# One load of 128 rows for each late half tile's queries, and a new table of issue times with a new order

## The chip, the cores and the metric

The kernel runs on one core of a Trainium2 chip. The core has a matrix engine (TensorE, PE in the profile), a vector engine (VectorE, DVE), an engine for activations (ScalarE, ACT), GpSimd (POOL), and a sync engine (SyncE, SP) whose queue issues all transfers of this kernel. Sixteen DMA engines move the data between memory and the core. The metric is the device time of one execution in microseconds, the median of several runs.

## What is computed

Local attention with block summaries, followed by a layer norm and a two-layer network with a residual:

```python
# q, k, v: (4, 8, 768, 64) float32
k_sum = k.reshape(B, H, nb, block, D).max(axis=3)     # block = 32
v_sum = v.reshape(B, H, nb, block, D).mean(axis=3)
scores_l = scale * np.matmul(q, k.transpose(0, 1, 3, 2))
mask_l = np.abs(pos[:, None] - pos[None, :]) < window  # window = 16
scores_s = scale * einsum('bhsd,bhnd->bhsn', q, k_sum) + np.log(block)
a = softmax over [where(mask_l, scores_l, -1e9), scores_s]
attn = np.matmul(a, concat([v, v_sum]))
x = attn.transpose(0, 2, 1, 3).reshape(B, S, 512)
xn = (x - mean) / sqrt(var + 1e-06) * g_ln
out = x + np.maximum(xn @ w_ch1, 0.0) @ w_ch2          # 512 -> 2048 -> 512
```

## The kernel before

**Tiles.** The 4 x 768 rows are 24 tiles T of 128 rows. A half tile t = 2T + hh holds four of the eight heads. The first batch (T = 0 to 5) takes an early path with float32 matmuls. The other three batches (T = 6 to 23, so 36 half tiles) take the late path, in which queries, keys, values and probabilities are split into a high and a low float16 part.

**Queries on the late path.** `load_q` (L602) loads the queries of one half tile. In memory they are 64 rows (the head dimension) of 512 float32 values (four heads by 128 positions), 2 KB a row. The tile `qs` has 128 rows, and its two halves hold the same 64 rows: `qhl` needs in its rows 0 to 63 the high part and in its rows 64 to 127 the low part. Two transfers of 64 rows, 128 KB each, fill `qs` from one source. Then ScalarE writes `qhl` as float16 of the scaled queries (128 x 512), and VectorE replaces rows 64 to 127 with the rest (64 x 512). `qs` has one buffer, so the next half tile's load waits until VectorE has read it. While batch 1's statistics are taken, that buffer also holds some of their loads (`stg`, L457). `qhl` has one buffer for each of two half tiles in turn.

**The rest of a half tile.** `load_k` (L615) loads keys (tile `ksg`) and splits them; `load_v` loads values (tile `vst`, three transfers) and splits them. `heads` (L640) makes the scores of both half tiles of T and the products with the values of tile T - 2, in one unbroken run of TensorE. `late_softmax` (L687) takes the maximum, the exponentials and their split, and transposes the probabilities with a DMA (tile `pt`). `batch_k`, `batch_q` and `batch_v` (L467 to L538) take the statistics of the next batch from loads into the one buffer `bst`. Layer norm transposes its result with a DMA too (tile `xt`), and `g1` and `g2` do the two layers (groups `h` and `a` in the profile) in groups of two tiles.

**Who sets the order.** Nothing is issued as the code is run through. A class `Plan` records every instruction with its dependences; `schedule` places them on five engines with a model of their times, and `issue` (L336) then emits them in order of the modelled start. The emitted order is fixed for each engine, SP's queue among them. Two inputs of the model matter here:

- `ISSUE`, `TURN` and `MOVE` (L114 on): the time that SP takes to issue a transfer (470 ns for every plain one, 1250 ns for a transpose) and, by the rows and bytes per row of its tile on the core, the time that it holds the DMA engines and the time from there to landing.
- `ORDER` (L54): 781 numbers, one for each step of the kernel (`load_q(12)`, `heads(6)` and so on), found by annealing, and added to the ranks by which `schedule` picks the next instruction (L346).

Every recorded instruction has line L356 in the profile, since it is emitted there. Groups are told apart by tile names.

Of the kernel before, what the change touches and what calls it, by code (L numbers as in the profile page):

```python
# [51 lines left out]
LAG = 2  # L52

ORDER = (  # L54
    "K>7dwc;Wy5hVTFXRmuPVjGF)d5XJxhoVEY|^{W5>ezgDpK(hb;yA%KbFy8<F(xw0ZzRCapFy8<FG_3#s!JGg8y)pm*AngDD=llQvM7sa~pVR;U"
    "qVNCzYC!-1Ug!V+)jR+Iwxs|6><0h<3oQTugvI~=zOeuQPX_=155fQcTZjMuji~?sfC>NrwI~1pvF-"
    "o=xWxbeDWw1Zhavy~c)kDs0ZIS>!ZrW^1p5E~n704_?~nig^$h?30zUu%OWyzgR?YwaOs)U_^RWN_eWw5az@z{FZ@mBi?uGyVUZem2ai#zNg{c"
    "4k^_Tzus-ge?T$lg<OsxO^%dP+aoRa_lkoW)pC!zoU>Z1Su42J*zf3pAol!yQS*tP%v8Ib?~CzSvHptt}3q2d4kHt+xc`@R4F7R~?vz0LpsH{A"
    "dKnyCN(dC&j<MEC#yq5J>;Hs}BULDm2NV9Edg@6rGNz8L@j-Sq$ev#J08LJR-^*i!%iIUWE2-o5|-"
    "nCAcgSgHU2Q#t?uV$A>l)BXSdK@<Q0=`;WU>qh_p4_E*I+0+03N8JDa9k>7g#GwEGn+X5_f13aQ$;to!&{O~bqq+b8UhV(?0doKVZ`l9;lm7qz"  # L60
    "Sk(Xj56S=k?JfWSl1cyowH5#X1^oa2e>wmF=EVR1?-"
    "u|7#@+w_(~<xG8w~&e1|t9fLr?$!W=jA7jcfn_5P1Lq5uE@3nLq#l=UM;&+}{8H9R&aYvj6}8v2p+azx@CIp#}f|WVrwTcA5YG=N|w7r=|b@Nk"
    "0Gp1ik<NJCy(bap3>|TCo5BUC#giIr;zpC6539A;JIusmTBTO%wnCpUwaO1q%QGS?T}(UI_pI!}kCGKh^*Ln;rlFxVHcQ>l6S0%@hCt)bIcQ5e"
    "EPOSqlIF`&s}1>0kf=1^EB}E4csvfS~{X+3ElPstN!A&C37(cjy2Ay^H_<$IAczzn%a8PMrV$Dq#Qs54`{XfY<;3?YsZ~jQ0Qkrv?B3IpF{QjO"
    "PFU$F2YW!T<mN;Kl#{xTydC6XpN^CK~_%!t?+CW8VM&m?QuIdKUlyG`;`-"
    "TgU(ZJ0t)ARZjo_R^k8u7^MII$F~3f>H`1(wkH4pD_j5ooCN>?CJq1q*NOlCI{E+q(!&4$JKF#MS<3(asmuTWix&U@^4S0XI<x=(c%=XTq80!E"
    "1dRXx_x1n(6<PoQ!1(|FlZ*fVR@(pnU>pDdArt@rJvsmY15^M2S3m#&(JBA{YbyW%3v2)YrYZmcWdZ;I1aJTVNiF~YKX?EDNBjT(2<`v>L|Xs="
    "Tp<7eHaP$QnX&)>;4c6G-a7yQX(a#v82|tOinIU!ZV><gB+dW-+@1gb9q<4Dz1{!+_DBE#EhPW|txNy_sLKEUKm-"
    "5)%&GtXdBp$!4!r;W8Uz3UBgFszR{#J1&gTFB@7(|YU=08OMz#O{PwM~w3L^jjyD<O&QWyXLEFJ&=&o2M~GHL(-#>oHw>|p=^B-"
    "a1`LgxSf=S2Vj1qlEEUjYCBAx;1Qdp-aFS{ncWU?%_o{0{&Cwm1L)2>t*6*2n+<#sB~REc*Zdvj6}9vp@g<Nk{+yjvD{~c-"  # L70
    "a5{Wf1@Xwr2nUur>eya!UXJUPk}`zHI;i>uvx50(t-djvD{~{!0J=Jsto6BtifH2U-9Cv`_#5w?+T}H6{Q6F+>0W7w-"
    "T6RyqIxI~o80flvSd&L02($}j)`e?0&I)c^nh3NHWvuo(aV+T{QL)baoSF24W&?=}DcIqm=d!twwA6S)8XGBp4I<6i&(vGM=^{^I}tQ1Ac$kk$"
    "YH1vmfzvcdoVRrde?$pQcX??C_naV!7;03QGV7100xg;M|k-"
    "v<By?JWQR1vCHvoX`LNnNI)!Qwab7c%T3OUG4w>L<Rr=(<%S}n9%?K3NruzoGbtUx=8>4U)=xyFaQ7mAHe_r*9-"
    "svyVw8!GNS+gDiZ(zDy{$j_ZI*FHv<3wzzP5Ww($S|T<ib;=)V8|BryO0OWXhdJ{SN1qVE6yMf?B%&msT-CqV!J2T1?`^-"
    "=%;ok0Kqd{F=ZT~7c2>^uMf$|C>(@W226$`Swobcp}|^z;A!_v`=v%O3y$yx;%--"
    "D&^;F)RQ87)1a8f6xE_@<;#x8?pcYVI%+mpV|Na3Z?)5OS}L7l)?Z1HRAvODMbJPn%)2ZWaR(<7cKw*69oVOtn~l?tP=nLysZEK650R%f(-"
    "xwozVaPLQDVvP-XxC$Lat7=(_*^E5`r-OY8stdf@;6(%Jw2vdRDdm!|*!B-"
    "a1`cL)FgXTSgd`1b$*trP$N^~(SMJ^%m!c+>y?3g!R*P^|y|2h9Kf6W0I#zUBY_=cfPv#FPL31eO2)`HTPm$UOi6m&O18%)tNuzU2S^1<wEfQq"
    "2GVUH||8(vScD1kL~doyq_Is0{!B<)Q!oR+az%(5?Uf*O~wS#i0NHHL?Hyu9g4)B&+}b@^=6L^G^T(*S-"  # L80
    "J$NWcI8@aq5nVVM8_R44!dp~?UM3IPBB_s9SLz`+0i?D_xy8m<5TD4_rU^{W5>xUv8L{3!qc6`TM6N3#F_0FM9vkc$8Rb^`zaT%rH}vc~`a?XC"
    "a+SG)iJ{@nlnn=t?YUabHBRk8p7!;%0073u%~0=obIA*28QI=lb>cAWqJ9nAm#HMal%#u@+sYt{e%&(Qz>D;xj-"
    "mX81bsm=fYLdyUDtf&9~BgX&#H^u+|+m`?TpA!H8Wc>gCTsQy#k#PV31110fN7n!UY^wkN7q0*RA-eznfh7O{VzdAMx6%LqOOF5l;U541m+Ali"
    "QcwT@lD7Z<{^|e!<r4q^@c94#NbLXr>KXt5F7^NazKZ|<sP6y&?2G^ZfDixxHH`oNye<F$8rA>*!<zs9GRgn{8sz`~P^ka^)W!e*8S4N4m!kjw"
    "^T7ZA86W@vM7aO|12+HwNHPEbjA#G=i?09wy7K@3`zinc)@%R(E<FGM`EmdNBQXE~@8JLcuP^`r&H?}cPALEY$j<-"
    "&=%D}qji~?sytV)TZVmtdNm2j+=Dq*_4JZHr@9h8oE7AY|(1`#4rJeu(^z8rtgX#bOcbNbGZ4UqdeboQ|3C{ojaGC%A{SN>DXXXF@TN?lX4GRD"
    "Oed+)I*uww+q4xj(CawSf8tDK3+Y<l)KVJX<Zn*#dzheLZT^axY!V~}i?p6Q*lurNvIxPSIYcl`<Z_)q%sG<M=VXOcD{3QSY6`BA4rM&<Dg{uG"
    "mw6p*J^rQd(Cno>^&`tmVQE&hNcSisKHbDRYk{18~iHraLgbx4!i;VyO=LrA+ftCONf29Ba;HCfn(YpWt?%V(W4p{&ITeScGL(2dEs*(Ty+r0n"
    "(RUH5T&d~q=(UJfEaE<@}FjxQp3aS79sqFv%u-O0qDwzNO^RNH^PqP325lR36h>`#Qsy6@tybS;VN4fw1v8Mn3It%~+Jf{Eup$-"
    "55{a^q9g8Kjen<fAN?$iJOpVa^VMDhRs&AR{pF5>_H%hdn>1)=}{d+7iFe=Pt2mgoQfIBNg^DUkpFk}d!MJ=OpJ;pYGU_=*4j;I;q%>c;>7@>u"  # L90
    "`?Ubg@L@T~v;9VGw&*;oJoyp#X`h>QRKi2MKlR+0bzv84b1kdFWVqvikqPOSg`F6saO^wj_Vk30YXGq(T#xeWjSQM3R5B=i6O8{_}~tiS*NW7_"
    "}!Kr;XUxhDVs-tYhak}d!M!@mFj3zPr<#JvCip&I}I16%+ADB1u29<u-cVUGX*6qEn|$5j9T!_@!(T)+SSVJiRttg8S2`1k++fx-"
    "X(Ru}*PCv^Y-L0<p>mMs7Ppwj>U94!C<A;SOvMyvn-Bs~BC88ZL?!NLFkyIcSO2Q&Zxeq8_ndKUlyD`)@!;#>d#K{5aU4jljhY#aapHB<lqv2g"
    "$Z=?nk>p+W!v$2b50HEsX^!%YAHekA|^rV;=EMF;=@<01e6Yb5{xo6i6LZ43YahB5#EpHct-"
    "4*387f<gcQaHaqM3&#Kdui^jyL0<p>dm{h<(7XTt73}~2AkqK-O1%I7RsjG2tS<lnAVvTHwe$b~eeD1Lk{<v7mZ|^$"
# [11 lines left out]
class Plan:  # L107
# [8 lines left out]
    MOVE = {
        "T": (1520.0, 550.0),
        (1, 2048): (170.0, 880.0),
        (128, 1024): (610.0, 490.0),
        (128, 1536): (680.0, 790.0),  # L120
        (128, 2048): (750.0, 880.0),
        (128, 2944): (1530.0, 960.0),
        (128, 3072): (1360.0, 1010.0),
        (128, 4096): (1770.0, 1290.0),
        (128, 576): (40.0, 2010.0),
        (24, 512): (110.0, 730.0),
        (32, 1024): (40.0, 820.0),
        (32, 2048): (40.0, 2000.0),
        (64, 1024): (220.0, 830.0),
        (64, 2048): (750.0, 770.0),  # L130
        (96, 1024): (490.0, 590.0),
        (96, 2048): (800.0, 700.0),
    }

    def __init__(self):
# [89 lines left out]
    def cost(self, engine, op, a, k, ins, outs):  # L225

        free = lambda x: math.prod(n for _, n in x.ap[1:])
        n = max(free(x) for x in ins + outs) if engine != "tensor" else free(a[0])
        if engine == "sync":
            x = (outs + ins)[0]  # L230
            size = mybir.dt.size(x.dtype)
            if "transpose" in op:
                return self.TURN, *self.MOVE["T"]
            return self.ISSUE, *self.MOVE[x.ap[0][1], free(x) * size]
        if engine == "tensor":
            dt = ins[-1].dtype
            if dt == F32R:
# [123 lines left out]
def body(ctx: ExitStack, tc, qt, qa, qe, kt, ks, va, vb, vs, g_ln, w1, w2, blocks, out):  # L361
# [5 lines left out]
    def work(tag, name, shape, dt=F32, bufs=1):  # L367
        return pl.tile(wp, shape, dt, tag, name, bufs)
# [21 lines left out]
    nc = pl  # L390
# [10 lines left out]
    sp = {}  # L401
# [199 lines left out]
    @pl.step  # L601
    def load_q(t):  # L602

        T, hh = divmod(t, 2)
        qs = stg('qs', [P, 4, P])
        for half in range(2):
            nc.sync.dma_start(qs[D * half : D * half + D], qt[T, hh])
        qhl = work(f"qhl{t % 2}", f"qhl{t}", [P, 4, P], F16)
        sc = bt["s", T // NT][:, 1:2]
        nc.scalar.activation(qhl[:], qs[:], AF.Copy, scale=sc)  # L610
        nc.vector.scalar_tensor_tensor(qhl[D:], qs[D:], sc[D:], qhl[D:], ALU.mult, ALU.subtract)
        st[t, "q"] = qhl
# [483 lines left out]
    for T in range(4, TT + LAG + 1):  # L1096
# [5 lines left out]
        b, i = divmod(T, NT)  # L1102
# [66 lines left out]
```

## Time and profile before

| | us |
|---|---|
| median of 3 runs | 632.35 |
| fastest and slowest of them | 631.36, 634.27 |
| the profiled execution | 631.18 |
| its span, first to last instruction | 629.4 |
| busy: TensorE, VectorE, ScalarE, GpSimd | 616.1, 401.6, 351.1, 147.0 |

The profile is of one execution. A group is named by its engine, its operation and the tiles that it writes and reads (`qhl<-qs`). "Busy" counts an engine's own instructions; SP's rows (SPq) are the times that its queue took to issue transfers. The chain of work is followed back from the last instruction, at each step to whatever released it. The table of stretches gives for each stretch the busy time of the engines, the granted TensorE clock, the mean busy share of the 16 DMA engines and what they moved in GB/s.

### The profile page before, as it was taken

What the parts mean: (1) busy time and instruction counts of PE and PEld (TensorE: products, weight loads), DVE (VectorE), ACT (ScalarE), POOL (GpSimd) and SP (SyncE); (2) the same over time, 40 slices, a digit from 0 to 9 for tenths busy, and PEclk for the clock granted to TensorE, in tenths of its full rate; (3) what the DMA queues carried; (4) which work ended last, traced back from release to release, by engine and by line L of the source; (5) the groups of instructions that cost most, each with busy time, mean ns of one, the idle gap of its engine ahead of it and who ended that gap; (6) DMA issues with size and microseconds to landing.
All of it is one profiled execution on the core that took longest, in us unless ns stands there. A gap on an engine that the chain in (4) does not pass through costs nothing.

```text
span 629.4 us, 14009 instructions
## 1 busy us (share of the span) xinstructions
PE 616.1 (98%) x5227; PEld 427.5 (68%) x5227; DVE 401.6 (64%) x1098; ACT 351.1 (56%) x926; POOL 147.0 (23%) x271
## 2 busy tenths in 40 slices
PE   8999999999999999999799999999999999999997
PEld 6777779885544676667377884577766756677754
DVE  4899999879668268846687465676877821171211
ACT  4898985459977257746677364565767711121100
POOL 4110302201333005403343022441433410030000
PEclk9999999999999999999799999999999999999999
DMA  9968798454797627555976426835776350011001
GB/s 285 308 175 259 237 302 231 99 159 120 192 226 166 151 73 191 155 159 134 199 209 139 95 70 125 188 83 146 176 152 151 74 120 0 1 48 23 1 25 43
DMA packets 115831, 89.52 MB, mean 142 GB/s; under 512 B 69553, under 2 KB 100273, under 8 KB 115762
## 3 DMA queue, kind: packets, MB, share of 16 engines
q1 hardware_dynamic: 115762, 88.61, 54.9%
q8 instruction: 41, 0.67, 0.4%
q14 instruction: 28, 0.23, 0.1%
HBM read 66.27 MB, written 6.29 MB: 115 GB/s over the span
## 4 chain that ended last, share of the span: by engine, by line
PE 60%; DMA 14%; ACT 10%; DVE 9%; SPq 4%; issue 2%; POOL 0%; ACTq 0%; DVEq 0%; POOLq 0%
PE h L356 26%; PE a L356 24%; SPq L356 4%; DMA bst<-in_ks 3%; DMA qs<-in_qt 3%; DMA bst<-in_vs 3%; PE o L356 3%; PE s L356 3%; DMA bst<-in_qa 2%; ACT p L356 2%; DVE m L356 2%; ACT bst L356 2%; PE low L356 1%; ACT w L356 1%; DVE kmax L356 1%
## 5 line engine op out<-in xcount | busy, mean ns | idle before, releaser
L356 PE MATMUL h<-xt,w_u 128*128 128x256 f16 x2304 | 264.5, 273 | 2.2 <-DVE h_x L356 2.2
L356 PEld LDWEIGHTS <-w_u 128*128 128x128 f16 x2304 | 224.8, 98 | 39.0 <-issue 5.0
L356 PE MATMUL a<-w,h_x 128*128 128x512 f16 (+1 forms) x960 | 211.8, 376 | 4.5 <-ACT h_x L356 4.1
L356 PEld LDWEIGHTS <-h_x 128*128 128x128 f16 x1008 | 98.0, 98 | 107.6 <-ACT h_x L356 5.1
L356 DVE SCALAR_TENSOR_TENSOR h_x<-h,h_x 128x512 f16<-128x512 f32 x80 | 54.1, 685 | 88.4 <-ACT h_x L356 88.3
L356 ACT ACTIVATE h_x<-h 128x512 f16<-128x512 f32 x80 | 46.2, 590 | 96.1 <-PE h L356 95.9
L356 ACT ACTIVATE p<-p,mn,sv 128x120 f32<-128x120 f32 x144 | 68.2, 475 | 12.6 <-POOL mn L356 12.3
L356 ACT ACTIVATE bst<-bst 128x384 f32<-128x384 f32 (+2 forms) x55 | 32.4, 589 | 52.3 <-DVE vsum L356 25.5
L356 POOL TENSOR_TENSOR p<-p,p 128x480 f16<-128x480 f32 x36 | 40.8, 1134 | 63.1 <-ACT p L356 52.4
L356 POOL TENSOR_TENSOR x<-x,rc 128x256 f32<-128x256 f32 x36 | 28.2, 789 | 94.5 <-DVE x L356 91.5
L356 PE MATMUL a<-w,h_y 128*128 128x512 f16 x192 | 43.6, 379 | 0.0
L356 POOL TENSOR_SCALAR mn<-mn,sv 128x4 f32<-128x4 f32 x36 | 19.2, 534 | 99.5 <-DVE mn L356 80.0
L356 DVE SCALAR_TENSOR_TENSOR m<-raw,m 128x512 uint32<-128x512 uint32 x64 | 42.1, 680 | 0.0
L356 DVE SCALAR_TENSOR_TENSOR qhl<-qs,sv,qhl 64x512 f16<-64x512 f32 x36 | 28.4, 788 | 18.9 <-ACT qhl L356 18.1
L356 DVE CUSTOM_DVE_ANT_0 p<-s,mask 128x120 f32<-128x120 f32 x144 | 33.4, 275 | 7.6 <-PE s L356 7.4
L356 ACT ACTIVATE qhl<-qs,sv 128x512 f16<-128x512 f32 x36 | 25.7, 714 | 19.8 <-DMA qs<-in_qt 14.8
L356 DVE SCALAR_TENSOR_TENSOR kl<-ksg,sv,kh 128x640 f16<-128x640 f32 x36 | 32.1, 891 | 7.3 <-ACT kh L356 6.9
L356 DVE SCALAR_TENSOR_TENSOR x<-a,scales,x 128x512 f32<-128x512 f32 (+1 forms) x24 | 17.7, 735 | 27.7 <-PE a L356 27.5
L356 ACT ACTIVATE kh<-ksg,sv 128x640 f16<-128x640 f32 x36 | 29.5, 821 | 6.9 <-DMA ksg<-in_kt 5.8
L356 PEld LDWEIGHTS <-h_y 128*128 128x128 f16 x192 | 18.7, 98 | 21.0
L356 DVE TENSOR_REDUCE x<-o 128x256 f32<-128x512 f32 x36 | 23.8, 684 | 9.1 <-PE o L356 9.1
L356 DVE SCALAR_TENSOR_TENSOR v<-vst,sv,v 128x512 f16<-128x512 f32 x36 | 29.2, 821 | 0.0
(116 smaller groups left out, 722.3 us busy)
## 6 DMA issues: line engine op xcount, KB each, us to landing
raw<-in_w SPq DMA_DIRECT2D x32, 512.0 KB
ksg<-in_kt SPq DMA_DIRECT2D x36, 368.0 KB
qs<-in_qt SPq DMA_DIRECT2D x72, 128.0 KB
out_x<-x SPq DMA_DIRECT2D x23, 256.0 KB
bst<-in_ks SPq DMA_DIRECT2D x20, 192.0 KB
bst<-in_qa SPq DMA_DIRECT2D x15, 256.0 KB
bst<-in_vs SPq DMA_DIRECT2D x20, 192.0 KB
vst<-in_va SPq DMA_DIRECT2D x36, 96.0 KB
```

Source lines behind the costliest of these rows:

```text
L356: getattr(getattr(nc, self.ops[i].engine), op)(*a, **k)
```

## The change

`load_q` issues one transfer for each half tile, which fills all 128 rows of `qs`. Its source is the 64 rows with a leading dimension of count 2 and step 0 put before them (`partition_broadcast(2)`), so the same rows are read twice. The scheduler's model no longer has one issue time for all plain transfers: each entry of `MOVE` now begins with its own issue time, and several other times in it are new. `ORDER` was annealed anew with that model.

```diff
 ORDER = (
-    "K>7dwc;Wy5hVTFXRmuPVjGF)d5XJxhoVEY|^{W5>ezgDpK(hb;yA%KbFy8<F(xw0ZzRCapFy8<FG_3#s!JGg8y)pm*AngDD=llQvM7sa~pVR;U"
...
+    "QSJZ#i{t<QdmR7(uHgUw&#wRfvEBdw8@m7hbEN<O60QIL*{}cq$Or%c?%V(W4v_!<=-"
...
 )
...
-    ISSUE, TURN, BEGIN, TICK, SWITCH, FIRST = 470, 1250, 1100, 10240 / 3, 93, 3500
+    BEGIN, TICK, SWITCH, FIRST = 1100, 10240 / 3, 93, 3500
     FLIGHT = 8
     MOVE = {
-        "T": (1520.0, 550.0),
-        (1, 2048): (170.0, 880.0),
-        (128, 1024): (610.0, 490.0),
-        (128, 1536): (680.0, 790.0),
-        (128, 2048): (750.0, 880.0),
-        (128, 2944): (1530.0, 960.0),
...
-        (64, 1024): (220.0, 830.0),
-        (64, 2048): (750.0, 770.0),
-        (96, 1024): (490.0, 590.0),
-        (96, 2048): (800.0, 700.0),
+        "T": (1320.0, 1450.0, 790.0),
+        (1, 2048): (400.0, 100.0, 1030.0),
+        (128, 1024): (400.0, 560.0, 690.0),
+        (128, 1536): (400.0, 540.0, 1100.0),
+        (128, 2048): (420.0, 850.0, 1060.0),
+        (128, 2944): (460.0, 1570.0, 940.0),
...
+        (64, 1024): (530.0, 360.0, 820.0),
+        (64, 2048): (545.0, 720.0, 920.0),
+        (96, 1024): (480.0, 460.0, 720.0),
+        (96, 2048): (410.0, 840.0, 780.0),
     }
...
             if "transpose" in op:
-                return self.TURN, *self.MOVE["T"]
-            return self.ISSUE, *self.MOVE[x.ap[0][1], free(x) * size]
+                return self.MOVE["T"]
+            return self.MOVE[x.ap[0][1], free(x) * size]
...
         T, hh = divmod(t, 2)
         qs = stg('qs', [P, 4, P])
-        for half in range(2):
-            nc.sync.dma_start(qs[D * half : D * half + D], qt[T, hh])
+        nc.sync.dma_start(qs[:], qt[T, hh].partition_broadcast(2))
         qhl = work(f"qhl{t % 2}", f"qhl{t}", [P, 4, P], F16)
```

The entries left out here change in the same way. Every transfer's bytes stay as they were, and the other engines' instructions are the same ones in another order.

More of the change, by code (lines that the diff above doesn't have):

```diff
@@ L54 @@
 ORDER = (
-    "K>7dwc;Wy5hVTFXRmuPVjGF)d5XJxhoVEY|^{W5>ezgDpK(hb;yA%KbFy8<F(xw0ZzRCapFy8<FG_3#s!JGg8y)pm*AngDD=llQvM7sa~pVR;U"
[L56 to L95, printed above, removed]
+    "QSJZ#i{t<QdmR7(uHgUw&#wRfvEBdw8@m7hbEN<O60QIL*{}cq$Or%c?%V(W4v_!<=-"
+    "2=M8TSAGExiB#Z?pgZ3q$|_Sr7mK@eBX}8;$?}KfnL~kJ|tLxm5rFG5Y`iSw#Q<y_x_28t4E2Z6E*u?5Y3%-"
@@ new lines @@
+    "k|^gx$yu04AcMrdX@kG<hlR<UHSk2`9S~xL>d49+r<C>thN9DU<CjGkJA7D^=SYA&Mg1{&msT-"
+    "2DJbGmWu!X;`#so4K@G(7|s9x2*&^a6P^G6;=lj@vi<-"
+    "6$EW}Q!N~vrJCXnY?3VxkBennk>5c#YfT;ifmD~USu8aTwp^N|jhPMCz*P;Lalmq|(UWWhw55)if`jP+tg5m%F4Tt~#ET{kf8IS+}n4kauYsLT"
+    "nyd(esaUK8w+Svd96Ab_W*T(<<CHnvW3XuQ*<In&9M)3dt`P2XZXx{(-"
+    "<mLbWqs0IJE$09Kg+TxSB+UQ+F}nZ%1RekYD{24$&JX|q^0fc|t;7HSag+c53>p9c0`UL;wlV+!y9EFMUm*Yh2}J+^C@ug1TH*iy@w)&2JfHvn"
+    "&Cvh<c=iAPMWp}#tLOj!L{0zzqo)7=2l4;^G+qDzg0uhsEjR!G!rTA<F5dtD{xbjo>1zN02Q&Zx02%-Q0cijL$0`5-"
@@ new lines @@
+    "sWJcn3j+WEhr<8=pD6$U;4uII%vk^c0$>0DeQW>#x>5iD)9?TPUt$0NGHU<;8p{9w_5=U`7zF?T)pP&=kR1R3h5P^iU&;Uf&$<8qtS<lnQ;h%r"
+    "|7-"
+    "vNbG85fT$2C)eCGfEJeB|ddZqvWNd5o+?uGyVf3pAoXW0M$wEqA9W(EKN7t#O!eB1y3t@r=`78L*h=;HtXqZ$AJ>$d;@;sO8wu<ZZ;&kq0qas&"
+    "VXpdSDL>2&}AYgPaNvEcvz?UVoip`ic&?eYKrSqcCEN3H+=;@<!Nf06(H6u|%gtiJ#M*^~eOa7zFH$kYG-BBB5P+pPcpuL}SGOcVeBgt7nsE7t"
+    "%2UXK6&vKIgVUDyBr%9{WGKJEYi4JZHrQUw42BLDyZmsS7(BVhmlLJt4{Iw}AFwkQAqb3Fh6kRt#9k^cYxE*}5@yA}Wd=2-"
+    "v$V{`xjn)3huLmmJCVW<E9(f0rUufYHRN)7-3pz;6z2-"
@@ new lines @@
+    "5%mFDn25wbTFq$EN@P9+&_BnF{~_;;#SyJmUZVhfDwf>G%KtZkGT5>;nJ*b`<~sCn*2`7E%BJT2=r6>R<o>XFLD^!e;;g!)pKlsw)5hM*si-tX"
+    "=>BtatzbFmC_=^ico+NH72Zi);V@BVhml2U!3By8r+H5_$jttzrNGpH%<=oF@PPjr;%qFBAX(bpQYVbie=qDN+Ccg+TxSDPsTtUK0QSgjoOpE0"
+    "F*HM@0Yt&ZqzXGt&S6jF<oa98&-Q2$TQ+1^xg3pWpxgg&zO_MJ50Mp56cd-s=DV<1PRI$u9r^Jp2Fuoh<+W+d}{V>1qG~W~KlC?q2`^yX*h|1-"
+    "}3P{Zs$|G7$g(u@wLS+c5wDHYxxB6eIuuX*>V`3<LlG{aye7zUTk{*2(|>zApd(`xF2G^a}t0ay9?}X+r=2WGw&y+o%8kzY+idYe@hANH72ZUr"
+    "PW015N+{*=Ya(;&=c6&}0Ar9{K<OXI}sS8VCRY=l}o!5_$jt-*x~1)j9wGJvjgXepCPeC-VRQmM{PS?F|3`V<rFq-WdP@BLe^cav}f#x#9o+bR"
@@ new lines @@
+    "hr$cpU%$y&M1lI2!-"
+    "}HKqUmA4mWIbhQ8fwAcUtOS}L7v>E^a8bAO5Vh#WRRQ3P=ORWF@p}GJ6z#RYpS)Kp?W7+@zOz;2yAS?g?1s?zauk`=_Ou_&E;a30vt^xo6ickO"
+    "m?=AoUa>W1t^IHG_6%GIZIlBM<gWv!EW=8-3d{+PfjkEv%_3i)vnJWMQzB2#-"
+    "`H=trd(;2_9E|_}Gadi{W3&JN=ZpXUMiKx3^{)T_Qv(119rFMGw+a9Nkk9}B@YetT@X7!GzZw7l6Ndl)(J}x4rpW*Q<>UYVrWXJJH!J`Eax4G<"
+    "Y$*T$DFFZgV(<U|K|KHfIVk`D{{H{}0i*x_``G{g1e^c=&gB39JG1})4kiEqh35bN^ico+91;KkhD-ne(6s;mRZai^u$uq>^V<LatGNIF5|ID@"
+    "E|CBKmYV<nTd)8B=pFz7(!&4$kE;Lwr5OMKm&E`7S>ylz6SV*TQk?()9JBxb)z$z1Q>*{~opS&HZc+dM6W{;;xaI%<aH;?QJk|gIQbqs(Zqfh$"
@@ new lines @@
+    "54->Wys!WNr}6*))%O4Y)sp}JXdeIo(h&dv>Ei$YLIMB)UHt$5f-V36N#6heLHPgwdFlWE@CX0^y$t{Wo$>$waJc{fO_u-"
+    "v%SQkJu<HN+ez^bt0~Y`QHKqUm;wk_Dp49*Uwafqin!Nx2kFo#%5*`2mhK&FJd$9liE0h2KHlhFj6^;M@m6!kjm!JRtPMiP#cvS!Z3rPR~mbd@"
+    "^G?M@S=h6TFWsm>=b_oCgxwHTO^!@+;FTDT%gvI~=eF^{o$f*DS{IdW5NSXitOTz#E6mS3l6utldArAlmtGECEBZvS0FCG8@BGdo>3Gx5`N1gx"
+    "wyDb0!7_|TYfl~kg`t<+*aq|EFx5EGbRvrKVoV@@40*3$pNY4NN4#5BacnbgkP{9BH;0*u(1tI_d@Av=zDm(xHI-mdlfx`d)PtgDWx(EOO;=KR"
+    "=YV`mAo{#_kmL32ALs0+#W@rEaS91UWi(CKz11$gmit_*e91s8i0NelnSsVZWfX)B^VlMyyqU`_wNoD{5Ao>6Q^GyH%^2`7K3LpRgCQ|?a-"
@@ new lines @@
+    "%bDkQ$+v(*-"
+    "8Ka@$LWrmZ|^$tQi0RFxmhAOLhPNi}(NkYj*$u|4RS>NH+igU+@3_&@TW0h{FH>LF51bvj_kH2)6(K?==7b%`pG~rj7sq&MyD}xjO&=QD6W72+"
+    "aTgcl!VT#2o+tnq&X~yc_@k?OOl<Q!4-fl+^$KMP~p27%cz*MQ8v35ZV9#)5!n-"
+    "TD|}ONR|Kp5;On+8+QNzrt<&)?;rpGsR9510nq>d(6RsjY7+neXgUA@E;j%Gk+1*%#XJB2VDSI{bL9X355oWdo)Z87lqCQFRYU*)T~Yu5X8ZsD"
+    "Wa<C^ocRC$c;Wy5R~rBT^9cX|YE%FKBhvr>Em;5nHWUB=??M0ocwPVimpT9dJwyNiAxQuLWxD_W%(nmkaF_r8+8qD@ZIb{0@4o;40Ez$qMXmq;"
+    "Cb<9qc^?1(fjs~K6-NL7bVC3DWcvUA$Pxem;*tOVo)!QAWuE{45kCL`X1D+USg`;9TciK~43+=?vBLlVd0GGfU8n#5z}f%*`I-"
@@ new lines @@
+    "O!y{Z5Ibm;&83DW=n35Ngwh`Im&Z$<zBN}vD#B_99)4aEQdyNUn*0hRy%?uGyVFZ2KZJeB|doihLc&glRD6te&S4vGK&$}Io@k*ELv6%YUb-"
+    "%J1i;nDy9Rp|f!<O2WzA&LM0wV(h0t+N0B2)zIQi_8E22%i7{B<27Aa2o&s;@JQH?;rpGqKN<h%o+dy9_9c4s_Os$I*I@P_00eOyuJVbx8DE%<"
+    ";?&8Hmd*s))xQ(?;`*JO{o9>@3{Z}s3`ydez^bt^~nGKN3s9^<KzGT$)NxL`@{eL4buPrfdT*kB&q-"
+    "ZCNKa1BiaA|h0Oo|^~V4IFx>zDp4I>Vo#g-"
+    "j+8Y1>lAQnl&n^G}<;Va32Gjrlg|YwthR^^1nq&X~Js<!8#jXGUUXlO*mFxfi$YcNjL<ax>q0s;Tv1<STP^AC==OF+9`R4!s#R>obc5?s#o=gA"
+    "$C1C&nupR&a;WPjMG|T`08qfd#Bx(Qvom>C_Y1jY%wOarHO*8-"
@@ L96 @@
+    "i+DHHZdB*?$b7lYl)+Yb}nPmU~SpEP1!qET!cr5?`v|#`M_u&8kzFz<UT?GIDY-"
+    "j)gay0+|*a!dsF75ySa^nC0(Fy<nfJXoTz1RQ$+b{qC3I6~8gf;*Gz_|baO)UTb3W@*!S*rj4l)3-"
+    "^d>#M*hb;gAdZqvWw*UYCU)TTtJc<ARt@Qu@gD3z1s5}4w;=2F;&iDWSSPlRH!jk|0"
 )
@@ L113 @@
     SAME = dict(tensor=0, vector=127, scalar=143, gpsimd=100, sync=0)
-    ISSUE, TURN, BEGIN, TICK, SWITCH, FIRST = 470, 1250, 1100, 10240 / 3, 93, 3500
+    BEGIN, TICK, SWITCH, FIRST = 1100, 10240 / 3, 93, 3500
     FLIGHT = 8
     MOVE = {
-        "T": (1520.0, 550.0),
-        (1, 2048): (170.0, 880.0),
-        (128, 1024): (610.0, 490.0),
-        (128, 1536): (680.0, 790.0),
-        (128, 2048): (750.0, 880.0),
-        (128, 2944): (1530.0, 960.0),
[L123 to L128, printed above, removed]
-        (64, 1024): (220.0, 830.0),
-        (64, 2048): (750.0, 770.0),
-        (96, 1024): (490.0, 590.0),
-        (96, 2048): (800.0, 700.0),
+        "T": (1320.0, 1450.0, 790.0),
[4 more added lines that the diff above has]
+        (128, 2944): (460.0, 1570.0, 940.0),
+        (128, 3072): (450.0, 1360.0, 1210.0),
+        (128, 4096): (430.0, 1660.0, 1470.0),
+        (128, 576): (500.0, 40.0, 1900.0),
+        (24, 512): (790.0, 100.0, 860.0),
+        (32, 1024): (600.0, 40.0, 1040.0),
+        (32, 2048): (500.0, 40.0, 1430.0),
+        (64, 1024): (530.0, 360.0, 820.0),
+        (64, 2048): (545.0, 720.0, 920.0),
+        (96, 1024): (480.0, 460.0, 720.0),
+        (96, 2048): (410.0, 840.0, 780.0),
     }
```

## The prediction, made before the changed kernel was run

> **What bounds the kernel now.** I read the page first: the span, the engines' busy time, and the shares of the chain that ended last.
>
> ```profile
> span 629.4 us, 14009 instructions
> PE 616.1 (98%) x5227; PEld 427.5 (68%) x5227; DVE 401.6 (64%) x1098; ACT 351.1 (56%) x926; POOL 147.0 (23%) x271
> PE 60%; DMA 14%; ACT 10%; DVE 9%; SPq 4%; issue 2%; POOL 0%; ACTq 0%; DVEq 0%; POOLq 0%
> ```
>
> TensorE is idle for only 629.4 - 616.1 = 13.3 us, so the change has little to win and very much to lose: whatever starves TensorE comes straight on top. The chain puts 14% on transfers and 4% on SP's queue, so attention's data does end last in places. Second, the table of stretches, cut where the late queries are loaded (three stretches of twelve half tiles, two pauses between them), and one stretch after them in which two output tiles leave and nothing else moves:
>
> ```profile
> core 0: us, PE busy (x) PEld busy (x) DVE busy (x) ACT busy (x) POOL busy (x), PEclk, DMA share, GB/s
> 550.50:554.50 4.00, 4.00 (x57) 3.19 (x57) 1.06 (x2) 0.53 (x1) 0.00 (x0) 1.00 0.36 135
> 109.00:211.00 102.00, 99.57 (x816) 63.16 (x814) 76.59 (x204) 69.02 (x173) 24.66 (x39) 1.00 0.66 163
> 211.00:235.00 24.00, 23.41 (x228) 17.30 (x227) 12.09 (x34) 9.43 (x22) 1.24 (x3) 1.00 0.32 96
> 235.00:351.00 116.00, 111.45 (x995) 74.08 (x993) 83.58 (x224) 79.08 (x209) 41.88 (x60) 0.97 0.69 168
> 351.00:371.00 20.00, 20.00 (x229) 17.41 (x227) 7.32 (x27) 6.00 (x10) 0.79 (x1) 1.00 0.16 40
> 371.00:490.00 119.00, 119.00 (x1098) 78.70 (x1096) 85.85 (x235) 72.93 (x184) 42.75 (x57) 1.00 0.65 147
> ```
>
> See two things. Between 109 and 371 us TensorE idles 2.4 + 0.6 + 4.6 = 7.6 us, and the clock of 0.97 over 116 us costs some 3.5 us more: about 11 us is all that a better order could win. And the 16 DMA engines are already busy for two thirds of each loading stretch. Third, one stretch of the chain in order of time (start, length, what), and what the tile views say of the queries and of a 128-row load:
>
> ```profile
> 182.73 4.34 DMA qs<-in_qt
> ...
> 187.09 0.73 ACT qhl L356
> ...
> 187.85 0.75 DVE qhl L356
> ...
> 189.18 2.43 DMA qs<-in_qt
> ```
>
> ```profile
> L356 SPq DMA_DIRECT2D qs<-in_qt x72: 471/479/1368, 109.1 to 486.3; - x72
> ...
>   DMA qs<-in_qt: 14.8, 12
> ```
>
> ```profile
> L356 SPq DMA_DIRECT2D bst<-in_qa x15: 328/343/543, 73.1 to 297.9; - x15
> ```
>
> The queries' tile has one buffer: load, ScalarE (0.73), VectorE (0.75), and only then the next load. ScalarE stood idle for a query load in 12 of 36 half tiles, 14.8 us in all. The queries come just in time; a load that lands later is felt at once.
>
> **The change part by part.** (a) Issue. 72 issues of 0.479 us become 36. A 128-row issue costs 0.343 us by the row of bst, and no 128-row load from a repeated source stands in the trace; I take 0.343 to 0.479, so SP gets back 36 x (0.958 - 0.41) = 20 us, spread over 377 us. SP's share of the chain is 4% (25 us), and only a part of it is queries: worth 0 to 5 us.
>
> (b) The transfer. It writes the same 256 KB, so at first sight nothing moves. But the source is a pattern of 2 copies (step 0) x 64 rows x 2 KB, and the question is over how many DMA engines it is dealt out. No transfer of before has such a source. What the trace does show is how others are dealt out, by the small packets that mark completion:
>
> ```profile
> DMA packets 115831, 89.52 MB, mean 142 GB/s; under 512 B 69553, under 2 KB 100273, under 8 KB 115762
> ...
> raw<-in_w SPq DMA_DIRECT2D x32, 512.0 KB
> ...
> pt<-p SPq DMA_TRANSPOSE x36
> xt<-x SPq DMA_TRANSPOSE x24
> vst<-vsum SPq DMA_DIRECT2D x24, 12.0 KB
> ...
> xn<-in_g_ln SPq DMA_DIRECT2D x1, 2.0 KB
> ```
>
> The 23 rows of that view (raw the first, xn the last) add up to 454 transfers. The 60 transposes move 256 KB each (tiles of 128 x 1024 in fp16); in pieces of 256 B these are 61,440 packets. Of the 69,553 under 512 B that leaves 8,113. With 16 marks for each of 369 plain transfers of 32 rows or more, 32 for a transpose, 12 for each of the 24 vsum transfers of 24 rows, and 1 for the single row of g_ln, it is 5,904 + 1,920 + 288 + 1 = 8,113, exactly; with 16 for all it would be 111 more. So I read that a transfer runs on as many engines, up to 16, as divide its outermost count: 12 for 24 rows, 1 for 1. Both sides of those transfers have one count, so they can't say what happens where the sides differ. But an engine must be given the same piece on both sides, and the source splits at its outermost count into 2 pieces of 64 rows. I take it that the new load runs on **two engines**, 64 rows of 2 KB each, instead of 16.
>
> The Trainium skill, "DMA: Bandwidth & Descriptors", sections "Why a DMA increments its semaphore by 16 and not by 1" and "Rules for kernel authors", states this: the number of engines is the largest up to 16 that divides the slowest dimension of both sides, and a leading zero-stride broadcast of c copies confines the DMA to at most c engines. The trace agrees for 24 rows and for one; no run here shows a broadcast yet. The same table speaks for the change too: two transfers to partition halves share the same engines, so use one of 128 partitions; by that rule alone the load would be spread as before.
>
> The price, if two engines. Alone, an engine moves 135 / 0.36 / 16 = 23.4 GB/s (stretch 550.5 to 554.5): 128 KB take 5.6 us. In the busy first stretch it is 163 / 0.66 / 16 = 15.4 GB/s: 8.5 us. Today's quickest half lands in 2.43 us, of which its 4 rows on each engine are 0.35, so 2.08 is fixed; the new load lands 7.7 us (to 10.6) after its issue began, where two quick halves need 0.5 + 2.4 = 2.9. I take 5.6 and 7.7, the row nearest to a state in which 14 engines have nothing of this load to draw.
>
> What that does to the two engines: the three loading stretches hold 0.66 x 102 + 0.69 x 116 + 0.65 x 119 = 225 us of work for each engine. Today's queries are 72 x 4 rows x 0.0875 us = 25 of it, leaving 200. The new loads add 36 x 5.6 = 202 on those two. 402 us of work stand against 337 us of time: 65 over, even if the two were never idle. The pauses (44 us, shares 0.32 and 0.16) have 33 us free, which could take some of it: 32 over. Every other transfer has a share on these two engines, so statistics, keys, values and transposes all wait behind the queries. The chain of one half tile says the same: 7.7 + 0.73 + 0.75 and the semaphores, about 9.3 us, with 3.7 us in which the two engines may serve the 200 / 36 = 5.6 us of others; 1.9 stay over, 11.2 us x 36 = 402. Bounds: if the others' work shrinks by 15.4 / 23.4 as contention goes, 132 + 202 = 334, nothing over; at 8.5 us a load, 187 + 306 = 493, 156 over. I take 55 us, between 32 and 65 and nearer the second, as a queue that waits in order won't keep two engines always fed.
>
> (c) SP's order. Behind a query load SP goes on to issue keys, values and statistics; behind the next load's wait for its one buffer everything queues, as now, but that wait ends some 4.8 us later in the quick case (7.7 against 2.9). TensorE's own order is fixed, so its score matmuls stall in line, and the matmuls of w1 and w2 behind them. The 139 us after 490 us are TensorE's own work and stay behind the last attention tile: a delay of the loading stretches reaches the end nearly whole. (d) The new table of issue times and the annealed order: the other transfers keep their bytes; a new order may win a share of the 11 us or lose as much. The table books the query load at the price of an ordinary 128-row one (0.42 + 0.85 + 1.06 = 2.3 us), so under (b) the order would place its reader some 5 us too early. I cost it at nothing beside (b).
>
> Sum, from the profiled execution (631.18 us: span 629.4 and 1.8 around it): + 55 gives 686. The median of the three runs stands 1.2 us above that execution: **687 us**.
>
> **The rivals.** *It does what it says*: the load spreads over 16 engines and lands in 2.1 + 8 x 0.0875 = 2.8 us. For it: the destination has 128 rows, and the counting above decided only cases with equal sides. SP gets 20 us back and the chain loses halves that wait for each other (4.34 us in the row above where 2.43 is possible). Half of the 11 us gives 626; all of it 621, nothing 632. This one ends on the faster side and decides wherever the source's outer count does not limit the engines: 18 in 100. *Two engines, but hidden*: in the row above the second half was issued at 182.73 and ScalarE took the tile at 187.09, and halves issued further apart can wait as long as the new load takes. If contention falls as in the lower bound (334 against 337) only late landings at the tight places are left, some 8 us: 640. Against it: 12 loads already end ScalarE's wait. 10 in 100. *Two engines at the loaded price*: 8.5 us a load and everything behind it, 156 over: 788. Against it: with 14 engines idle the crowd is gone. 6 in 100. My forecast, 645 to 760, keeps 66.
>
> **How the numbers follow.** A measurement of this kernel tells about 0.5% (3.2 us) from no change. Faster by more: most of the first rival, 0.11. Within: the rest of it and the edge of the second, 0.08. Slower: the forecast, the third and most of the second, 0.81. The range for 8 in 10 takes the forecast's own 645 to 760, the hidden case below it, and ends at 630, where most of the first rival begins; above 760 lies the loaded price. 0.06 and about 0.12 are left out.
>
> **What would show it.** With two engines: packets under 512 B fall by far more than the 36 x 16 marks of the halves that vanish, to 69,553 - 72 x 16 + 36 x 2 = 68,473 (68,977 with 16 engines); the mean DMA share stays near 0.55 while the loading stretches grow; rows "DMA qs<-in_qt" of 7 us and more in the chain, and ScalarE's wait for them well above 14.8 us; TensorE's idle time grows by about what the span does. Wrong would be: 68,977 marks and query rows under 4 us. If marks say two engines but the span grows by under 15 us, my sizes for contention failed, not the mechanism. SP's query issues should be 36 either way.

## The result, and the profile after

The change made the kernel slower: 727.56 us in the median of four runs (721.12 to 730.04) beside 631.93 before (a fourth run has joined the three), a ratio of 1.149 (95% interval 1.141 to 1.157; the two medians alone give 1.151). The forecast was 687, in a range of 630 to 760. Of all executions below, one of 1287 us (the first run with 64 rows outermost) stood far outside its fellows, and its profile is not read. The page of the changed kernel, the lines that answer to those shown of before (span, busy time, the granted clock in 40 slices, the packets, and the chain by engine and by line):

```profile
span 726.6 us, 13949 instructions
PE 641.8 (88%) x5227; PEld 436.9 (60%) x5227; DVE 400.6 (55%) x1098; ACT 351.6 (48%) x926; POOL 149.3 (21%) x271
PEclk9999999998989999999989989998999999999999
DMA packets 114751, 89.50 MB, mean 123 GB/s; under 512 B 68474, under 2 KB 99194, under 8 KB 114683
q1 hardware_dynamic: 114682, 88.61, 57.3%
DMA 35%; PE 34%; DVE 13%; ACT 10%; issue 5%; SPq 2%; POOL 1%; ACTq 0%; DVEq 0%; POOLq 0%
DMA qs<-in_qt 19%; PE h L360 14%; PE a L360 10%; DMA bst<-in_vs 5%; DMA bst<-in_qa 4%; ACT p L360 4%; DMA bst<-in_ks 3%; DVE qhl L360 2%; PE low L360 2%; PE s L360 2%; PE o L360 2%; SPq L360 2%; DVE x L360 2%; ACT qhl L360 1%; DVE m L360 1%
```

The same bytes move and the other engines do the same work (VectorE 400.6, ScalarE 351.6), but transfers now hold 35% of the chain instead of 14%, the query loads alone 19%. Packets under 512 B are 68,474: with two engines 68,473 were forecast, with sixteen 68,977. (In the packet records one of the 68,474 is not of SP's queue, so SP's own are the 68,473 of the forecast.) The records also show it directly: exactly two packets are under way at once for 80.7 us of the span, where it was 7.4 before. By TensorE's account the 97.2 us of span are 726.6 - 641.8 - 13.3 = 71.5 us more idle time and 25.7 us more busy time for the same matmuls. The mean DMA share is 57.3%, hardly more than the 54.9% before, but it is a share of a longer span: 0.573 x 726.6 = 416 us for each engine instead of 0.549 x 629.4 = 346, for the same bytes. The stretches, cut where the query loads of the changed kernel run (the two short ones are the pauses):

```profile
core 0: us, PE busy (x) PEld busy (x) DVE busy (x) ACT busy (x) POOL busy (x), PEclk, DMA share, GB/s
119.00:257.00 138.00, 107.86 (x753) 63.68 (x751) 67.75 (x175) 69.51 (x173) 25.55 (x39) 0.91 0.60 121
257.00:276.00 19.00, 17.63 (x169) 12.64 (x169) 11.04 (x32) 8.06 (x18) 1.87 (x4) 0.91 0.22 65
276.00:433.00 157.00, 128.41 (x1089) 85.77 (x1088) 83.52 (x224) 78.66 (x210) 41.34 (x58) 0.93 0.71 127
433.00:447.00 14.00, 13.14 (x140) 8.66 (x139) 8.47 (x28) 5.42 (x11) 1.75 (x3) 1.00 0.24 71
447.00:600.00 153.00, 138.33 (x1226) 92.84 (x1225) 84.12 (x234) 75.12 (x186) 38.34 (x54) 0.96 0.68 111
```

The loading stretches took 448 us instead of 337, and in them TensorE idles and its granted clock is 0.91 to 0.96. The third view is the chain in order of time, the fourth the queries' tile (issues: shortest, median, longest ns, first and last start; then who sat idle before its readers, and how often):

```profile
276.50 8.49 DMA qs<-in_qt
285.02 0.73 ACT qhl L360
285.78 0.75 DVE qhl L360
...
287.22 8.05 DMA qs<-in_qt
...
303.30 5.72 DMA bst<-in_ks
...
311.89 7.78 DMA bst<-in_ks
```

```profile
L360 SPq DMA_DIRECT2D qs<-in_qt x36: 520/576/607, 119.1 to 590.1; - x36
...
  DMA qs<-in_qt: 108.2, 25
```

Query loads now take about 8 us where the rows of before had 2.43 and 4.34; ScalarE waits for them 25 times in 36, 108.2 us in all (14.8 before). And loads of statistics, whose own shape is untouched, take 5.7 and 7.8 us behind them, where the chain of before has 2.3 to 4.1 for these loads between 109 and 303 us. SP's queue itself stands still for query loads too, before and after (who, for what, us in total, times, longest):

```profile
SPq L356 <- DMA qs<-in_qt: 6.5, 6, 3.2
SPq L360 <- DMA qs<-in_qt: 36.5, 13, 5.8
```

First to last issue of the queries grew from 377 to 471 us.

What the slow loads do to others shows best in the transposes. All 61,440 packets of 256 B are theirs. In the packet records they take 47.0 ns in the mean, 26.6 before (the median is 18 in both); for each of the 16 engines that is 180.5 us instead of 102.0, which is more than the whole growth of 70 us. From 316 to 319 us, behind the query load issued at 309.50, some 18 of these packets are under way all the time, and beside them about two others at once: 48 GB/s move in these 3 us, and TensorE is busy for 0.76 us. It looks as if a transpose holds all sixteen engines until the two that are behind reach their part of it. The records name no engine, so that reading is not shown.

### The profile page after: what moved, and what is told of

It is laid out like the page before. It is cut to its first block, busy times and chain, and to the rows that moved or that the text cites. A ratio compares the mean times of both kernels' runs of the same rounds, so it can differ in the third digit from the quotient of the medians.

```text
span 726.6 us, 13949 instructions
## 1 busy us (share of the span) xinstructions
PE 641.8 (88%) x5227; PEld 436.9 (60%) x5227; DVE 400.6 (55%) x1098; ACT 351.6 (48%) x926; POOL 149.3 (21%) x271
## 2 busy tenths in 40 slices
DMA packets 114751, 89.50 MB, mean 123 GB/s; under 512 B 68474, under 2 KB 99194, under 8 KB 114683
## 3 DMA queue, kind: packets, MB, share of 16 engines
q1 hardware_dynamic: 114682, 88.61, 57.3%
## 4 chain that ended last, share of the span: by engine, by line
DMA 35%; PE 34%; DVE 13%; ACT 10%; issue 5%; SPq 2%; POOL 1%; ACTq 0%; DVEq 0%; POOLq 0%
DMA qs<-in_qt 19%; PE h L360 14%; PE a L360 10%; DMA bst<-in_vs 5%; DMA bst<-in_qa 4%; ACT p L360 4%; DMA bst<-in_ks 3%; DVE qhl L360 2%; PE low L360 2%; PE s L360 2%; PE o L360 2%; SPq L360 2%; DVE x L360 2%; ACT qhl L360 1%; DVE m L360 1%
## 5 line engine op out<-in xcount | busy, mean ns | idle before, releaser
L360 PE MATMUL h<-xt,w_u 128*128 128x256 f16 x2304 | 280.8, 282 | 40.1 <-DVE h_x L360 23.6
L360 PEld LDWEIGHTS <-w_u 128*128 128x128 f16 x2304 | 231.9, 101 | 87.2 <-issue 34.1
L360 PE MATMUL a<-w,h_x 128*128 128x512 f16 (+1 forms) x960 | 219.0, 382 | 20.6 <-ACT h_x L360 10.3
L360 ACT ACTIVATE qhl<-qs,sv 128x512 f16<-128x512 f32 x36 | 25.8, 717 | 108.2 <-DMA qs<-in_qt 108.2
L360 POOL TENSOR_TENSOR p<-p,p 128x480 f16<-128x480 f32 x36 | 41.4, 1153 | 109.8 <-ACT p L360 60.9
L360 PE MATMUL a<-w,h_y 128*128 128x512 f16 x192 | 45.1, 387 | 8.3 <-DVE qhl L360 3.4
L360 POOL TENSOR_TENSOR x<-x,rc 128x256 f32<-128x256 f32 x36 | 26.3, 739 | 75.8 <-DVE x L360 75.2
L360 ACT ACTIVATE kh<-ksg,sv 128x640 f16<-128x640 f32 x36 | 29.5, 819 | 17.6 <-DMA ksg<-in_kt 10.8
L360 DVE TENSOR_REDUCE vsum<-bst 96x16 f32<-96x512 f32 x20 | 13.6, 678 | 36.0 <-DMA bst<-in_vs 35.8
L360 DVE SCALAR_TENSOR_TENSOR x<-xn,rs,x 128x512 f16<-128x512 f32 x24 | 18.9, 787 | 22.5 <-ACT x L360 22.3
L360 POOL TENSOR_SCALAR rs<-mv 128x1 f32<-128x1 f32 x24 | 12.8, 533 | 87.4 <-DVE mv L360 79.2
```

Source lines behind the costliest of these rows:

```text
L360: getattr(getattr(nc, self.ops[i].engine), op)(*a, **k)
```

## The experiments

The theory: the load runs on two engines because its source has outermost count 2. First the change was taken apart, and the source was changed in two ways that bring the count to 64 or 128.

**The order and the table alone.** The two loads of 64 rows are put back under the new table and order.

```diff
-        nc.sync.dma_start(qs[:], qt[T, hh].partition_broadcast(2))
+        for half in range(2):
+            nc.sync.dma_start(qs[D * half : D * half + D], qt[T, hh])
```

> The new table and the new order with the two loads of 64 rows put back. Theory (the load runs on two engines and nothing else is wrong): the order and table are worth a few us either way, 620 to 640 us, query loads of 2.4 to 5 us. Rival (the new order is what costs the 96 us, the load little): 700 us or more.

Measured: 628.39 us beside 630.53, ratio 0.998 (0.995 to 1.000). The order does no harm; what it may win can't be told from nothing.

**The load alone**, under the old table and order:

```diff
-        for half in range(2):
-            nc.sync.dma_start(qs[D * half : D * half + D], qt[T, hh])
+        nc.sync.dma_start(qs[:], qt[T, hh].partition_broadcast(2))
```

> The old table and order with the one load from the repeated source. Theory: nearly all of the loss is here, 700 to 740 us, with query loads of about 8 us and 68,474 packets under 512 B. Rival (the new order is to blame): within 10 us of before. A third case, that the old order hides part of it because it places the reader later: 650 to 690 us.

Measured: 748.08 us, ratio 1.189 (1.181 to 1.197). The load is the loss, and a little more of it than expected: over the two halves it costs 118 us under the old order (748.08 against 630.53) and 99 under the new (727.56 against 628.39). The third case, that the old order hides a part, is excluded.

**The same rows laid out twice in memory.** The host writes each half tile's 64 rows twice, as it already does for the keys, and the load has a plain source of 128 rows. The order is that of after.

```diff
     qT = qT.transpose(0, 4, 1, 3, 2, 5).reshape(TT, 2, D, 4, P)
+    qT = np.concatenate([qT, qT], axis=2)
...
-        nc.sync.dma_start(qs[:], qt[T, hh].partition_broadcast(2))
+        nc.sync.dma_start(qs[:], qt[T, hh])
```

> After, with the 64 rows laid out twice in memory by the host, so that one load of 128 rows has a plain source; same order, same bytes moved, same number of issues. Theory: the load spreads over 16 engines, lands in 2.5 to 5 us, 68,977 packets under 512 B, time 620 to 635 us. Rival (one load in place of two, or the order that counts on it, is the cost): 700 us or more.

Measured: 618.65 us (618.3 to 619.66) beside 630.53, ratio 0.983 (0.979 to 0.987). It is faster than before and after. From its page, its queries' tile and the stretch in which they are loaded:

```profile
span 616.5 us, 13949 instructions
PE 610.6 (99%) x5227; PEld 426.5 (69%) x5227; DVE 403.4 (65%) x1098; ACT 352.4 (57%) x926; POOL 153.4 (25%) x271
DMA packets 115254, 89.51 MB, mean 145 GB/s; under 512 B 68977, under 2 KB 99697, under 8 KB 115186
```

```profile
L360 SPq DMA_DIRECT2D qs<-in_qt x36: 327/346/616, 117.6 to 483.1; - x36
...
  DMA qs<-in_qt: 4.3, 4
```

```profile
117.00:486.00 369.00, 368.95 (x3321) 248.91 (x3321) 256.33 (x690) 236.12 (x593) 112.16 (x156) 1.00 0.61 150
```

The marks are those of sixteen engines, to the packet. TensorE does not idle at all while the queries are loaded, at full clock. So the idea of the change is sound: one load in place of two is worth 628.39 - 618.65 = 9.7 us under this table.

**The repeated source with the 64 rows outermost.** This keeps the step of 0 but puts it inside.

```diff
-        nc.sync.dma_start(qs[:], qt[T, hh].partition_broadcast(2))
+        nc.sync.dma_start(qs[:], qt[T, hh].unsqueeze(1).to_broadcast([D, 2, 4, P]))
```

> After, with the source still repeated with step 0 but 64 rows outermost and the 2 copies inside; the rows so land in another order in the tile, so that the scores are of other values. Theory (the outermost count of 2 is the cause, not the repetition): as with plain rows, 620 to 635 us and loads of 2.5 to 5 us. Rival (a repeated source is slow in itself, two reads of one row for instance): about 727 us with loads of 8 us.

> The repeated source with 64 rows outermost once more, for its profile (scores of other values, as before): 68,977 packets under 512 B, loads of 2.5 to 5 us, 620 to 624 us; an issue of 0.59 us where the plain rows take 0.35.

Measured: 622.25 us (0.987, 0.983 to 0.992), and 620.76 when it was run again (0.984, 0.981 to 0.987). The profile shown is that of the second run, with 68,977 packets under 512 B and loads of 3.5 us in the mean. A repeated source isn't slow in itself. Its issues are longer, as expected, and it ends within 2 to 4 us of the plain rows:

```profile
L360 SPq DMA_DIRECT2D qs<-in_qt x36: 562/590/935, 118.8 to 484.1; - x36
```

**Outermost counts of 2, 4 and 8, nothing repeated.** The host writes the rows twice and leaves a gap of one row after each 64, 32 or 16, so that the source can't be one run of 128 rows. For 4:

```diff
+    qT = np.concatenate([qT, qT], axis=2).reshape(TT, 2, 4, P // 4, 4 * P)
+    qT = np.pad(qT, ((0, 0),) * 3 + ((0, 1), (0, 0)))
...
-        nc.sync.dma_start(qs[:], qt[T, hh].partition_broadcast(2))
+        nc.sync.dma_start(qs[:], qt[T, hh, :, : P // 4])
```

> The 64 rows laid out twice by the host with a gap after each 64, so that the source has outermost count 2 and nothing is repeated; order, issues and bytes as after. Theory (the outermost count alone sets it): loads of about 8.2 us and 720 to 735 us, as after. Rival (step 0, the same rows read twice, is part of the cost): faster than after by more than 10 us.

> The same with a gap after each 32 rows, outermost count 4. Theory (four engines of 32 rows each): loads of 2.1 + 32 x 0.0875 = 4.9 us, 68,473 + 2 x 36 = 68,545 packets under 512 B; the four engines have 200 + 101 = 301 us of work in 337 us of loading stretches, so the engines no longer set the pace: 625 to 640 us. Rival (what counts is how late one load is, in proportion): 618.65 + 109 x (4.9 - 2.8) / (8.2 - 2.8) = 661 us.

> The same with a gap after each 16 rows, outermost count 8. Theory: loads of 3.5 us, 68,689 packets under 512 B, 618 to 624 us. Rival in proportion to the load: 633 us.

Measured, with the landing worked out from the trace's semaphore records (start of the issue to the last completion mark, mean of 36):

| outermost count | packets under 512 B | landing us | time us | ratio to before (95%) |
|---|---|---|---|---|
| 2, repeated (after) | 68,474 | 8.3 | 727.56 | 1.149 (1.141 to 1.157) |
| 2 | 68,473 | 8.2 | 719.74 | 1.143 (1.138 to 1.147) |
| 4 | 68,545 | 6.2 | 658.71 | 1.048 (1.043 to 1.053) |
| 8 | 68,689 | 4.6 | 627.86 | 0.998 (0.996 to 1.000) |
| 128 (copied rows) | 68,977 | 3.2 | 618.65 | 0.983 (0.979 to 0.987) |

The packet counts are the expected ones to the packet, and with count 4 exactly four packets are under way at once for 41.9 us of the span (8.2 before). A count of 2 makes the loss without any repetition; the step of 0 adds nothing that these runs can tell (8 us between medians of different sets, and the two intervals overlap). But the sizes fit neither expectation at 4 and 8: the theory said 625 to 640 and 618 to 624, the rival 661 and 633. The landings themselves were forecast too short, 4.9 and 3.5 us. The curve bends. From 3.2 to 4.6 us of landing a microsecond costs the kernel 9.2 / 1.4 = 6.6 us, from 4.6 to 6.2 it costs 19, from 6.2 to 8.2 it costs 31, nearly one for each of the 36 loads. It may be that the first microsecond falls mostly into slack and the last finds none; but the engines' backlog grows along with the landing, so the curve can't say which of the two is paid for. With four engines ScalarE's wait is already there, though my sum left those engines 36 us free:

```profile
L360 SPq DMA_DIRECT2D qs<-in_qt x36: 546/600/632, 118.8 to 526.2; - x36
...
  DMA qs<-in_qt: 57.7, 22
```

**Is it the late query load, or the queue behind it?** Three runs tried to part the two. The first gives the model nearly the measured price (7.6 us to landing, where the records have 8.3), so that the order expects the queries late. The model still books the sixteen engines together for 0.85 us; it knows of no backlog on two.

```diff
             if "transpose" in op:
                 return self.MOVE["T"]
+            if "qs" in x.tensor.name and ins == []  and len(a[1].ap) > 2 and a[1].ap[0][0] == 0:
+                return 575.0, 850.0, 6200.0
             return self.MOVE[x.ap[0][1], free(x) * size]
```

> After, with the repeated load priced in the model as it was measured (issue 0.575, 0.85 of the engines, 6.2 to landing) and the table of ranks as it is. Theory (two engines full and a load that holds its one buffer for 8.2 us: an order can't give them back): 690 to 730 us. Rival (the loss is mostly an order that places the readers 5 us too early): under 660 us.

Measured: 698.17 us (1.109, 1.104 to 1.114), as the theory had it: an order that knows the price wins back 29 of the 109 us that lie between after and the copied rows, or 22 against the plain source of count 2, which was run in the same set. The ranks were not annealed anew for it. ScalarE then hardly waits for queries (of true_price, the queries' tile):

```profile
L362 SPq DMA_DIRECT2D qs<-in_qt x36: 536/574/612, 110.5 to 575.2; - x36
...
  DMA qs<-in_qt: 8.4, 7
```

The second gives the tile two buffers. To make room, the ring that holds relu's results is one shorter.

```diff
-        return work(tag, f"{tag}{stg_n[0]}", shape, dt, 1 + (tag == "xn"))
+        return work(tag, f"{tag}{stg_n[0]}", shape, dt, 1 + (tag in ("xn", "qs")))
...
-RAW, YB, MB = 4, 2, 2
+RAW, YB, MB = 4, 1, 2
```

> After, with two buffers for the queries' tile, so that a load can be issued a half tile earlier (the ring of relu's results one shorter). Theory A (full engines): 690 us or more. Theory B (late landing into one buffer): most of the loss goes, 630 to 660 us.

Measured: 750.73 us (1.189, 1.186 to 1.193), 23 us above after. Theory B falls, for the shorter ring, which is in the run too, can't account for the rest: the control below, with the same ring and an extra load, stands only 24 us above the copied rows. By the same 24 us it isn't shown that two buffers are worse than one. The wait for queries is down to 19.1 us; instead, the keys are waited for (54.0 us, 10.8 in after), and some statistics a little longer (42.6, 35.8 in after) (of two_buffers, the queries' tile and the table of waits: who, for what, us in total, times, longest):

```profile
L360 SPq DMA_DIRECT2D qs<-in_qt x36: 508/566/629, 109.4 to 574.7; - x36
...
  DMA qs<-in_qt: 19.1, 5
```

```profile
ACT kh L360 <- DMA ksg<-in_kt: 54.0, 14, 9.6
...
DVE vsum L360 <- DMA bst<-in_vs: 42.6, 10, 9.5
```

The third loads the queries on sixteen engines and puts a load that nobody reads behind each, once from a plain source and once from the repeated one.

```diff
-RAW, YB, MB = 4, 2, 2
+RAW, YB, MB = 4, 1, 2
...
-        nc.sync.dma_start(qs[:], qt[T, hh].partition_broadcast(2))
+        nc.sync.dma_start(qs[:], qt[T, hh])
+        nc.sync.dma_start(work("unread", f"unread{t}", [P, 4, P])[:], qt[T, hh, :D].partition_broadcast(2))
...
+    qT = np.concatenate([qT, qT], axis=2)
```

This is the second of the two; the control has `qt[T, hh]` as the source of its unread load.

> Queries laid out twice by the host and loaded on 16 engines, and behind each of the 36 loads a second load of 256 KB from the same place into a tile that nobody reads (for its 2 KB a row the ring of tiles that hold relu's results is one shorter). The control of the next run: 36 x 256 KB = 9.4 MB more to move and 36 more issues. Both theories: 620 to 640 us.

> As the run before, but the unread load comes from the repeated source with outermost count 2. The queries themselves are not late by their own transfer; whatever is lost against the control is what two filled engines do to everything queued behind. Theory A (two full engines are most of the loss): 670 to 720 us. Theory B (the loss follows how late the one-buffer query load lands, as outer4 suggests): within 20 us of the control.

Measured: 642.64 us for the control, a little above its range, and 807.5 for the other. The 165 us between them lie outside both theories, and they are not the answer: the unread tile has one buffer too, and SP, which issues in order, stood still until the previous unread load had landed. The table of SP's waits in extra_load:

```profile
SPq L360 <- DMA unread<-in_qt: 191.6, 34, 8.0
```

So this run shows what a slow load costs when SP's queue itself waits for it, and doesn't measure the two engines alone.

What the two others leave: whether the queries are waited for 108, 19 or 8 us, first to last issue takes 471, 465 and 465 us, some 13 us for each half tile, against 365 us with sixteen engines. That looks like the pace of two full engines, but the packet records say otherwise. In the 448 us of the loading stretches of after, no packet of SP's queue is under way for 73 us and only one for 5, so the two engines can't have been busy together for more than 370. Nor is the pace the same under every order: load_alone takes 505 us. From the first query issue to 8.3 us after the last, two or more packets are under way for 372 to 385 us in all five runs with a count of 2 (outer2, two_buffers, true_price, after, load_alone), and for 262 us with the copied rows; what is left, 94 to 128 us, passes with at most one packet. So the backlog of two engines is not the whole pace: for a part of the time they moved nothing either. How the 109 us divide between late queries, the queue behind them and SP's waits stays open: the runs that took away one made another longer.

## Why the prediction was right, and where its size was off

**Two engines, read from the marks: right.** The forecast read the rule of outermost counts from the 24-row and one-row transfers and carried it over to a case where the two sides differ. The count of marks (68,473 forecast, 68,474 measured), the runs with counts 2, 4 and 8, and the repeated source with 64 outermost all bear it out. The Trainium skill says the same in "DMA: Bandwidth & Descriptors", section "Rules for kernel authors", and these runs agree with it. The advice of that table to use one transfer of 128 partitions holds as well, where the source has 64 or 128 rows outermost: the copied rows won 9.7 us over two halves.

**The price of one load: right for two engines.** 7.7 us was taken, 10.6 at worst; the chain shows 8.05 and 8.49, the records a mean of 8.3. The same working (2.1 us fixed and 0.0875 for each row) gave 4.9 and 3.5 for four and eight engines, and 6.2 and 4.6 were measured. So its split into a fixed part and rows is not confirmed, and there was some luck in how close it came for two.

**The issue: a little off.** 0.343 to 0.479 us was taken; it is 0.576 for the repeated source and 0.346 for plain rows. SP got back 36 x (0.958 - 0.576) = 14 us instead of 20.

**What the two engines do to the loading stretches: right in kind, too small.** The term of the sum was 55 us, from 402 us of work against 337 of time, less what the pauses would take in. The three stretches came to 448 us, 111 over, and the pauses gave back 11 of it. The step that was mis-sized is how well two engines with 402 us of work can be kept fed. The forecast let them be busy nearly all the time; the records leave at most 370 of the 448 us in which both can have been. It also kept the others' work at 200 us for each engine or let it shrink, since fourteen engines would be free of the queries. For the transposes it went the other way: the time of their packets grew from 102.0 to 180.5 us for each engine. And the 55 us counted on some of the pauses' free 33 us; 11 came. (The stretches of after hold 11, 12 and 13 loads, not twelve each; the sum goes over all 36 and stays.)

**The clock: a term that was missing.** TensorE's busy time grew by 25.7 us for the same 5227 matmuls, at a granted clock of 0.958 instead of 0.995. The clock accounts for it: busy time by clock is 641.8 x 0.958 = 615 and 616.1 x 0.995 = 613. Over the runs the clock goes down as TensorE's idle time goes up: 1.000 with 5.9 us idle (copied rows), 0.982 with 35.6 (count 4), 0.971 with 60.9 (true price), 0.958 with 84.8 (after), 0.896 with 150.0 (extra_load). The forecast expected the idle time to grow by about what the span does; it grew by 71.5 of 97.2 us. It counted the throttle only as something to win (3.5 us), not as what follows when TensorE is made to wait. How much of it would have been idle time otherwise isn't known, so it isn't simply to be added to the 71.5 us.

**The new order: costs nothing, right.** order_alone stands at 0.998. But the order's belief in a quick load matters once the load is slow: the true price is worth 22 to 29 us, and I had put it at nothing beside the rest.

**The first rival did not come about; where the load does spread, its best case holds.** 626 was given, and 621 if all of the 11 us came back; the copied rows are at 0.983 of before, which is 621.6 on the scale of the 632.35 that the forecast started from (618.65 in their own set). They leave TensorE idle for 616.5 - 610.6 = 5.9 us of the whole span, where 13.3 stood before.

## What to carry to other kernels

Before two transfers are merged, look at the outermost count of both sides of the new one: put a large dimension outermost (64 and 128 ran on sixteen engines here, 24 on twelve, and 8 still cost 9 us), or lay the data out so that there is one; a leading dimension of 2 turned a load of 3 us into one of 8. Count the small packets of the page: they tell over how many engines the transfers ran, when the mean share of 16 engines hardly moves. And price a slow transfer by what is queued behind it, and by the clock, which fell as TensorE waited, not by its own lateness alone; and don't take two backlogged engines to be busy all the time (here at most 370 of 448 us).

## What the runs showed of the hardware that was not expected

SP's issue time goes with the source's shape, not only with its rows: 0.346 us for 128 plain rows, 0.576, 0.600 and (outer8) 0.658 us for 2 x 64, 4 x 32 and 8 x 16, and 0.590 for 64 x 2 with the step of 0 inside. The transposes' issues can stretch when two engines are behind: the tile view of the probabilities has 1260 ns in the median before and 2094 after, so SP's queue loses time there too. It depends on the order as well, for true_price has 1286 in the median and 3795 at most. Before and after:

```profile
L356 SPq DMA_TRANSPOSE pt<-p x36: 1231/1260/2057, 157.1 to 509.5; - x36
L360 SPq DMA_TRANSPOSE pt<-p x36: 1232/2094/3769, 178.3 to 633.1; - x36
```

And in extra_load, where TensorE waits longest, the granted clock falls furthest, to 0.896 in the mean and to five tenths in one slice:

```profile
PEclk8967799787776685899999999999999999999999
```
